# Row halves of an M2 tile between the score bursts of the first three quads

## The chip, the cores and the metric

The kernel runs on one core of a Trainium2 chip. The metric is the device time of one execution in microseconds (us); shorter is better. The core has a matrix engine (TensorE, "PE" in the profile, its weight loads "PEld"), a vector engine (DVE), an activation engine (ACT), a general engine (POOL) and a queue engine (SP). Each works through its own instructions in order, and semaphores tie them together.

## The reference

Attention with a decay, for 8 batches, 8 heads, 576 positions and 64 channels, and behind it a two-layer SiLU network on 4608 tokens of 512 channels:

```python
scores = scale * np.matmul(q, k.transpose(0, 1, 3, 2))
cum = np.cumsum(np.log(np.clip(f, 0.0001, 1.0)), axis=-1)
decay = cum[:, :, :, None] - cum[:, :, None, :]
scores = np.where(causal, -1000000000.0, scores + decay)   # causal: the upper triangle
attn = softmax(scores)
x = (attn @ v)  # as (4608, 512)
h = x @ w_in                       # 512 -> 2048
g = h * (1.0 / (1.0 + np.exp(-h)))
out = g @ w_out                    # 2048 -> 512
```

## The kernel before

**The numbers.** Everything that TensorE multiplies is bf16. The decay is taken apart: V, and a column of ones beside it, are multiplied by a weight per position (`convert_v`, L410, on POOL), so that the exponential of the scaled score, masked, is all that is needed, and the column of ones gives the divisor.

**The stages.** The first 128 positions of every batch are done ahead, up to about 62 us. The other 448 of each batch go by pairs of heads: 4 pairs in a batch, 32 in all. Two pairs are a **quad**; the loop at L952 runs quads m = 0 to 15, and pairs n = 2m and 2m + 1 belong to quad m.

**A pair.** `scores` (L445) is called three times per pair, with c = 0, 1, 2. Each call multiplies K by Q for both heads of the pair into one of two PSUM score buffers, and ACT takes the exponential (L471, L465). The contraction has 64 rows, so one head uses rows 0 to 63 of TensorE and the other rows 64 to 127, at the same time (64\*128 in the profile). Calls 0 and 1 each give one "wide" exp (1024 columns); call 2 gives a "tail" exp (L465, 640 columns) and a "short" one (256 columns). `mask` (L475) and `mask_tail` (L481) zero the upper triangle on DVE. `attend` (L491) multiplies by V into `dn`: 18 matmuls at L507 and 10 at L516 with all 128 rows, then DVE divides (L524, L525). `back` (L532) transposes the output of a whole quad into the layout that the network needs: for quads 3 to 14 by two DMAs of SP, for the others (0, 1, 2 and 15) by seven TensorE transposes (L549) and two copies on DVE (L552, L555).

**The network.** Tokens are in groups of 256, 384 or 512 columns. **M1** (`m1_chunk`, L561): a group has 16 chunks; a chunk is four matmuls into `hp` (L568), a Tanh on ACT (L576) and a product on DVE (L577) into `gt`. **M2** (`m2_part`, L595): 128 tokens are a tile; a tile is four parts of four 512-wide matmuls into `po` (L613), then an eviction on ACT (L623), then a store from POOL's queue. `hp`, `po`, `pr`, `dn` and `tx` share four PSUM buffers; a new one takes the buffer that has been free longest.

**Row halves.** `m2_rows` (L630) does half an M2 tile: 32 matmuls of 64 rows and 256 columns, two at a time, one on each half of TensorE's rows, into two PSUM buffers `pr`. Half 0 and half 1 exchange the two buffers. Between them `m2_fence` (L648) makes DVE read one column of `pr`, and with it half 1 waits for half 0. `m2_out` (L652) evicts by two DVE instructions (L656). Before the change quads 4 to 15 use it.

**The order** around the change is written out in the loop. A quad has three bursts of scores: (n; 0, 1), (n; 2) with (n+1; 0), and (n+1; 1, 2). In the old form `slot` puts M1 chunks and M2 parts behind each burst, and both attends follow. In the row form the halves of one tile stand between the bursts, then come the first attend, some chunks, the second attend and more chunks. `whole` (L905) first ends an M2 tile that is begun, and returns the next one if it can be had whole. `fill` and `plan` choose between M1 and M2 and count their cost as columns; `slot` also issues the stores that were open when it began, and `passed` counts slots, after some of which a group becomes ready for M1. `turn` and `prepare` issue the casts on POOL (L400, L404), the transposes of Q and K (L428) and the loads of later pairs on SP's queue.

Of the kernel before, what the change touches and what calls it, by code (L numbers as in the profile page):

```python
# [18 lines left out]
def kernel(  # L19
# [80 lines left out]
    def xg(g):  # L100
        if g not in xgs:
            tag, bufs = {4 * P: ("x4", 1), 2 * P: ("x2" if g < 3 else "xt", 2), RB: ("x3", 3)}[GW[g]]
            xgs[g] = xpool.tile([P, NCC, GW[g]], BF16, name=tag, tag=tag, bufs=bufs)
        return xgs[g]
# [45 lines left out]
    def head(p, i):  # L150
        return p // 2 * 4 + 2 * i + p % 2
# [337 lines left out]
    BY_DMA = [3 <= m < NQ - 1 for m in range(NQ)]  # L489

    def attend(n):  # L491
        b, p = divmod(n, NP)
        if p % 2 == 0:
            xqs[n // 2] = xqp.tile([P, NGR, 2, D], BF16, name="xr", tag="xr", bufs=3)
        xq = xqs[n // 2]
        u, ut = us.pop(n), uts[n % 4]
        dn = pbig.tile([P, NGR, D + 1], FP32, name="dn", tag="big")

        def vals(kb, i):
            h = head(p, i)  # L500
            return v0[b][:, h, :] if kb == 0 else vbf[b][:, kb - 1, h, :]

        for i in range(2):
            for c in range(1, NM):
                for kb in range(c + 1):
                    o = AT[c, kb]
                    nc.tensor.matmul(  # L507
                        dn[:, i * NR + c - 1, :],
                        lhsT=u[:, i, o : o + P],
                        rhs=vals(kb, i),  # L510
                        start=(kb == 0),
                        stop=(kb == c),
                    )
        for i in range(2):
            for kb in range(NM + 1):
                nc.tensor.matmul(  # L516
                    dn[:, NGR - 1, :],
                    lhsT=ut[:, kb, i : i + 2, :].rearrange("p i t -> p (i t)"),
                    rhs=vals(kb, i),
                    start=(i == 0 and kb == 0),  # L520
                    stop=(i == 1 and kb == NM),
                )
        rec = recp.tile([P, NGR], FP32, name="rec", tag="rec")
        nc.vector.reciprocal(out=rec[:, :], in_=dn[:, :, D])  # L524
        nc.vector.tensor_tensor(  # L525
            out=xq[:, :, p % 2, :],
            in0=dn[:, :, 0:D],
            in1=rec[:, :, None].to_broadcast([P, NGR, D]),
            op=ALU.mult,
        )  # L530

    def back(m):  # L532
        b, c0 = m // 2, m % 2 * 2
        xq = xqs.pop(m)
        g, t0 = TAILS_OF[b]
        xr = xg(REST_OF[b])[:, c0 : c0 + 2, :]
        xt = xg(g)[:, c0 : c0 + 2, :].rearrange("p i t -> p (i t)")[:, t0 * P : (t0 + 1) * P]
        if BY_DMA[m]:
            nc.sync.dma_start_transpose(
                out=xr.rearrange("p i (a q) -> p (i a) q", q=P),  # L540
                in_=xq[:, 0 : 2 * NR, :, :].rearrange("p c w d -> p (c w d)"),
            )
            nc.sync.dma_start_transpose(
                out=xt[:, None, :], in_=xq[:, 2 * NR, :, :].rearrange("p w d -> p (w d)")
            )
            return
        tx = pbig.tile([P, NGR, P], BF16, name="tx", tag="big")
        for c in range(NGR):
            nc.tensor.transpose(  # L549
                tx[:, c, :], xq[:, c, :, :].rearrange("p w d -> p (w d)"), ident_bf[:, :]  # L550
            )
        nc.vector.tensor_copy(  # L552
            out=xr, in_=tx[:, 0 : 2 * NR, :].rearrange("p (i a) q -> p i (a q)", i=2)
        )
        nc.vector.tensor_copy(out=xt, in_=tx[:, 2 * NR, :])  # L555
# [33 lines left out]
    def store(n):  # L589
        n = max(n, 0)  # L590
        for q_, dst, src in stores[:n]:
            q_.dma_start(out=dst, in_=src)  # L592
        del stores[:n]
# [54 lines left out]
    def m2_fence(g, tb):  # L648

        nc.vector.tensor_copy(out=fence[:, :], in_=pos[g, tb][1][:, 0:1])  # L650
# [22 lines left out]
    at = {"m1": 0, "m2": 0, "left": 0.0}  # L673
# [23 lines left out]
    def step(force=0):  # L697

        a, c = at["m1"], at["m2"]
        want = wanted(a, c)  # L700
        if not want:
            return None
        g1 = M1[a][0] if a < len(M1) else NG
        g2 = M2[c][0] if c < len(M2) else NG
        can1 = g1 in ready and not (M1[a][1] == 0 and g1 > g2 + lag["g"])
        can2 = open2["w"] and c < len(M2) and g2 < g1
        kind = force if (force == 1 and can1) or (force == 2 and can2) else want
        if kind == 1:
            if M1[a][1] == 0:
                begin[g1] = (0, c)  # L710
            m1_chunk(g1, M1[a][1])
            at["m1"] += 1
            t = 4 * (GW[g1] / 2.4 + 2.5)
        else:
            m2_part(*M2[c])
            at["m2"] += 1
            t = 4 * (DM / 2.4 + 2.5)
        return t

    def behind():  # L720
        t = sum(4 * (GW[g] / 2.4 + 2.5) for g, _ in M1[at["m1"] :] if g in ready)
        t += sum(4 * (DM / 2.4 + 2.5) for g, _, _ in M2[at["m2"] :] if g in ready)
        return t / 1000
# [158 lines left out]
    def turn(n):  # L882
        if 0 < n < NU - 2:
            cast_qk(n + 2)
            transposes(n + 2)
# [19 lines left out]
    def whole():  # L905

        while at["m2"] < len(M2) and M2[at["m2"]][2] and wanted(at["m1"], at["m2"]):
            t = step(2)
            at["left"] -= t / 1000
        c = at["m2"]  # L910
        while M1[at["m1"]][0] in ready and M1[at["m1"]][1] >= NFC - 4 and M2[c][0] == M1[at["m1"]][0]:
            at["left"] -= step(1) / 1000
        a = at["m1"]
        if c >= len(M2) or M2[c][2]:
            return None
        g1 = M1[a][0] if a < len(M1) else NG
        return M2[c][:2] if M2[c][0] < g1 else None

    LAG, LOW = 13.0, 2.0
    QUAD = [10.9] * (NQ // 2) + [11.7] * (NQ // 2)  # L920

    def spent():
        t = sum(4 * (GW[g] / 2.4 + 2.5) for g, _ in M1[: at["m1"]])
        return (t + at["m2"] * 4 * (DM / 2.4 + 2.5)) / 1000
# [15 lines left out]
    def passed():  # L940
        for x in pending:
            x[0] -= 1
        while pending and pending[0][0] == 0:
            ready.update(pending.pop(0)[1])

    def slot(us_, least=0, ends=(0, 0)):
        n = len(stores)
        fill(us_, least, ends)
        store(n)
        passed()  # L950

    for m in range(NQ):  # L952
        n = 2 * m
        piece = 1.7 if m < 2 else 2.4
        if m == 2:
            assert at["m2"] >= M2_OF[0]
            first_pool.__exit__(None, None, None)
            gpools[0] = ctx.enter_context(tc.tile_pool(name="third", bufs=1))
            lag["g"] = 2
        if m == 4:  # L960
            lag["parts"] = 12
        goal = (spent() if m <= 4 else goal) + QUAD[m]
        rows = whole() if m > 0 and BY_DMA[m - 1] else None
        scores(n, 0)
        scores(n, 1)
        turn(n)
        if m > 0:
            back(m - 1)
            if m % 2 == 0:
                b = m // 2 - 1  # L970
                pending.append([2, [REST_OF[b]] + ([TAILS_OF[b][0]] if b == NM - 1 else [])])
        prepare(n)
        if rows:
            at["m2"] += 4
            m2_rows(*rows, 0)
            m2_fence(*rows)
            mask(n)
            scores(n, 2)
            scores(n + 1, 0)
            turn(n + 1)  # L980
            prepare(n + 1)
            m2_rows(*rows, 1)
            mask_tail(n)
            mask(n + 1)
            scores(n + 1, 1)
            scores(n + 1, 2)
            m2_out(*rows)
            passed()
            attend(n)
            mask_tail(n + 1)  # L990
            slot(1.9, 3)
            attend(n + 1)
            slot(1.8)
            rest(goal)
            at["left"] = 0.0
            continue
        slot(piece, 0, (1, 0))
        mask(n)
        scores(n, 2)
        scores(n + 1, 0)  # L1000
        turn(n + 1)
        prepare(n + 1)
        slot(piece, 0, (1, 0))
        mask_tail(n)
        mask(n + 1)
        scores(n + 1, 1)
        scores(n + 1, 2)
        mask_tail(n + 1)
        slot(piece, 0, (1, 0))
        attend(n)  # L1010
        attend(n + 1)
        slot(min(3.5, max(0.8, behind() - LAG)) if m > 1 else 0.8)
# [39 lines left out]
```

## Time and profile before

| | |
|---|---|
| median of 3 runs | 340.42 us (340.25 to 346.89) |
| the profiled execution | 340.37 us, its span 338.6 us |
| granted TensorE clock, mean | 0.998 |
| M1 matmuls (L568), busy | 123.0 us |
| M2 matmuls (L613 full rows, L639 halves), busy | 93.8 and 46.0 us |
| score matmuls (L460), busy | 27.8 us |

Quads, from the first score of one to the first score of the next, and the busy time of the engines in them:

| quad | from, to (us) | length | PE | DVE | ACT | POOL |
|---|---|---|---|---|---|---|
| 0 | 62.46 to 71.85 | 9.39 | 9.13 | 4.55 | 7.52 | 5.99 |
| 1 | 71.85 to 82.44 | 10.59 | 10.59 | 7.06 | 8.44 | 3.26 |
| 2 | 82.44 to 96.88 | 14.44 | 14.44 | 7.34 | 9.67 | 7.69 |
| 3 | 96.88 to 109.99 | 13.11 | 13.11 | 9.22 | 10.48 | 7.33 |
| 4 | 109.99 to 124.16 | 14.17 | 14.17 | 7.96 | 9.05 | 3.31 |
| 5 | 124.16 to 137.56 | 13.40 | 13.38 | 9.93 | 10.54 | 7.34 |

How to read it: matmuls are pipelined, and the busy time of one reaches over the start of the next, so a TensorE that is "busy" can still be slower than it could be. The distance from one start to the next is what counts. In the chain of waits a line gives the start, the length and what took it; in a timeline it gives the start, the time from the first start to the last end, the engine, the line, the operation, the shape and the count.

### The profile page before, as it was taken

How to read it: one execution, taken by the hardware profiler on the slowest of the kernel's cores; microseconds unless marked ns; L12 is line 12 of the kernel's file. 1: busy time of each engine (PE TensorE's matmuls, PEld its weight loads, DVE VectorE, ACT ScalarE, POOL GpSimd, SP SyncE). 2: the span in 40 equal slices, each digit the busy share in tenths (PEclk: the TensorE clock that was granted, in tenths of full speed). 3: DMA queues.
4: the chain of work that ended last, by engine and by line, in shares of the span. 5: the costliest groups of instructions: out<-in, count | busy, mean ns of one | idle time of the engine just before them, and what ended most of it. 6: DMA issues, size and time to landing. Idle time of an engine off the chain costs nothing.

```text
span 338.6 us, 10066 instructions
## 1 busy us (share of the span) xinstructions
PE 331.8 (98%) x4136; PEld 223.0 (66%) x4136; DVE 193.1 (57%) x423; ACT 216.7 (64%) x389; POOL 131.1 (39%) x227
## 2 busy tenths in 40 slices
PE   8999999999999999999999999999999999999995
PEld 3745665577656767858767796867777685555654
DVE  4765735275467458656656965775685564333330
ACT  5757636676767767848748794875877583344331
POOL 8986317823618227316332721821652000001011
PEclk9999999999999999999999999999999999999999
DMA  8999999999679699979769979797998200101112
GB/s 155 194 186 223 184 199 167 249 205 186 150 182 214 155 205 162 154 174 177 185 149 200 182 136 210 154 201 146 206 157 138 60 33 14 50 33 39 58 58 66
DMA packets 142462, 50.75 MB, mean 150 GB/s; under 512 B 133328, under 2 KB 139728, under 8 KB 142416
## 3 DMA queue, kind: packets, MB, share of 16 engines
q1 hardware_dynamic: 132400, 32.93, 56.4%
q0 software_dynamic: 9856, 17.04, 21.5%
q8 instruction: 32, 0.52, 0.7%
q10 hardware_dynamic: 160, 0.13, 0.1%
q14 instruction: 14, 0.11, 0.1%
HBM read 36.85 MB, written 9.44 MB: 137 GB/s over the span
## 4 chain that ended last, share of the span: by engine, by line
PE 93%; DMA 2%; DVE 1%; ACT 1%; issue 1%; POOL 1%
PE hp L568 36%; PE po L613 25%; PE pr L639 12%; PE sc L460 7%; PE dn L507 6%; PE dn L516 3%; DMA w_in_bf<-in_moe_w_in_dram 2%; PE tp L286 2%; PE wm L233 1%; DVE gt L577 1%; PE tx L549 1%; POOL vf L141 1%; DVE xq L375 0%; PE sc L320 0%; ACT th L576 0%
## 5 line engine op out<-in xcount | busy, mean ns | idle before, releaser
L577 DVE SCALAR_TENSOR_TENSOR gt<-th,hp 128x384 bf16<-128x384 bf16 (+2 forms) x208 | 107.0, 522 | 74.6 <-ACT th L576 66.2
L576 ACT ACTIVATE th<-hp 128x384 bf16<-128x384 f32 (+2 forms) x208 | 96.4, 470 | 73.9 <-PE hp L568 72.3
L568 PE MATMUL hp<-x,w_in_bf 128*128 128x384 bf16 (+2 forms) x704 | 123.0, 321 | 0.9 <-DMA w_in_bf<-in_moe_w_in_dram 0.5
L568 PEld LDWEIGHTS <-w_in_bf 128*128 128x128 bf16 x832 | 78.8, 98 | 49.8 <-issue 0.8
L613 PE MATMUL po<-w_out_bf,gt 128*128 128x512 bf16 (+1 forms) x400 | 93.8, 371 | 0.0
L471 ACT ACTIVATE u<-sc 128x1024 bf16<-128x1024 f32 (+1 forms) x96 | 74.7, 818 | 7.0 <-PE sc L460 7.0
L613 PEld LDWEIGHTS <-gt 128*128 128x128 bf16 x400 | 37.6, 98 | 32.5 <-issue 0.2
L592 POOL DMA_DIRECT2D out_dram<-osb x38 | 20.9, 551 | 87.3 <-ACT osb L623 36.5
L414 POOL TENSOR_TENSOR vp<-vf,w_bf 128x520 bf16<-128x520 f32 (+1 forms) x32 | 34.1, 1067 | 36.7 <-DMA vf<-in_v_dram 30.3
L639 PE MATMUL pr<-w_out_bf,gt 64*128 64x256 bf16 x768 | 46.0, 269 | 0.0
L639 PEld LDWEIGHTS <-gt 64*128 64x128 bf16 x768 | 38.6, 94 | 2.8
L400 POOL CAST qkb<-qf 128x384 bf16<-128x384 f32 x32 | 18.1, 566 | 48.4 <-DMA qf<-in_q_dram 47.7
L623 ACT ACTIVATE osb<-po 128x512 f32<-128x512 f32 (+1 forms) x25 | 14.6, 584 | 26.6 <-PE po L613 22.7
L460 PE MATMUL sc<-qkT 64*128 64x128 bf16 (+1 forms) x640 | 27.8, 206 | 0.3 <-ACT u L471 0.3
L477 DVE TENSOR_TENSOR u<-u,tri 128x768 bf16<-128x768 bf16 x32 | 21.3, 666 | 7.7 <-ACT u L471 7.6
L460 PEld LDWEIGHTS <-qkT 64*128 64x128 bf16 x640 | 20.0, 94 | 8.2 <-issue 6.2
L465 ACT ACTIVATE ut<-sc 128x640 bf16<-128x640 f32 x32 | 22.6, 708 | 1.9 <-PE sc L460 1.7
L400 POOL CAST qkb<-kf 128x384 bf16<-128x384 f32 x32 | 17.5, 545 | 16.5 <-DMA kf<-in_k_dram 16.4
L507 PEld LDWEIGHTS <-u 128*128 128x128 bf16 x576 | 20.6, 98 | 2.9
L507 PE MATMUL dn<-vp,u 128*128 128x65 bf16 x384 | 21.8, 194 | 0.0
L525 DVE TENSOR_TENSOR xr<-dn,rec 128x448 bf16<-128x448 f32 x32 | 20.0, 625 | 1.1
L507 PE MATMUL dn<-v,u 128*128 128x65 bf16 x192 | 20.0, 194 | 0.0
(72 smaller groups left out, 244.0 us busy)
## 6 DMA issues: line engine op xcount, KB each, us to landing
out_dram<-osb POOLq DMA_DIRECT2D x32, 256.0 KB, 3.0
vf<-in_v_dram SPq DMA_DIRECT2D x26, 256.0 KB, 4.7
qf<-in_q_dram SPq DMA_DIRECT2D x64, 96.0 KB, 3.4
kf<-in_k_dram SPq DMA_DIRECT2D x64, 96.0 KB, 3.2
w_in_bf<-in_moe_w_in_dram POOLq DMA_DIRECT2D x4, 512.0 KB, 7.8
w_out_bf<-in_moe_w_out_dram POOLq DMA_DIRECT2D x4, 512.0 KB, 8.4
vf<-in_v_dram POOLq DMA_DIRECT2D x6, 256.0 KB, 9.8
qkb<-in_q_dram POOLq DMA_DIRECT2D x8, 128.0 KB, 5.3
```

Of the source, the lines that this page charges most:

```text
L400: nc.gpsimd.tensor_copy(out=t2[:, c0 : c0 + NR, :].rearrange("p c x -> p (c x)"), in_=t[:, :, :, :].rearrange("p c h d -> p (c h d)"),)
L414: nc.gpsimd.tensor_tensor(out=vbf[b][r, c, :, :], in0=vst[b][c][r, :, :], in1=w_bf[r, c + 1, b * H : (b + 1) * H, None].to_broadcast([n, H ...
L460: nc.tensor.matmul(sc[:, i, o : o + q1 - q0], lhsT=kt, rhs=t[r, q0:q1], start=True, stop=True)
L465: nc.scalar.activation(out=ut[:, :, 0:3:2, :].rearrange("p k i t -> p i k t"), in_=sc[:, :, T0 : T0 + (NM + 1) * ST].rearrange("p i (k t) ...
L471: nc.scalar.activation(out=u[:, :, c * SM : c * SM + w], in_=sc[:, :, 0:w], func=ACT.Exp, scale=scale)
L477: nc.vector.tensor_tensor(out=x, in0=x, in1=tri[:, None, None, :].to_broadcast([P, 2, NR, P]), op=ALU.mult)
L507: nc.tensor.matmul(dn[:, i * NR + c - 1, :], lhsT=u[:, i, o : o + P], rhs=vals(kb, i), start=(kb == 0), stop=(kb == c),)
L568: nc.tensor.matmul(hp[:, :], lhsT=w_in_bf[:, cc, fc * P : (fc + 1) * P], rhs=xcols(g, cc), start=(cc == 0), stop=(cc == NCC - 1),)
L576: nc.scalar.activation(out=th[:, :], in_=hp[:, :], func=ACT.Tanh, scale=0.5)
L577: nc.vector.scalar_tensor_tensor(out=gt[:, fc, :], in0=th[:, :], scalar=1.0, in1=hp[:, :], op0=ALU.add, op1=ALU.mult,)
L613: nc.tensor.matmul(po[:, :], lhsT=gt[:, fc, tb * P : (tb + 1) * P], rhs=w_out_bf[:, fc, m0:m1], start=(fc == 0), stop=(fc == NFC - 1),)
L639: nc.tensor.matmul(pos[g, tb][y], lhsT=gt[r, fc, tb * P : (tb + 1) * P], rhs=w_out_bf[r, fc, y * DM // 2 : (y + 1) * DM // 2], start=(half ...
```

## The change

For quads 0 to 3 the loop now asks `whole` for a tile too. Where it returns one, the quad takes the row form. There `back` of a quad that is transposed by TensorE (`late`) is called behind the first attend and not behind the first burst. In quads 0 and 1 the chunks between and behind the attends are exactly four and two M1 chunks (`ones`, new); in quads 2 and 3 they are chosen by `slot`, and the end of these quads is a slot with a bound of its own. From quad 4 on the written order is the same, and only the share of M1 and M2 in each quad moves.

```diff
@@ -943,6 +943,14 @@
         while pending and pending[0][0] == 0:
             ready.update(pending.pop(0)[1])
 
+    def ones(k):
+        n = len(stores)
+        for _ in range(k):
+            step(1)
+        at["left"] = 0.0
+        store(n)
+        passed()
+
     def slot(us_, least=0, ends=(0, 0)):
         n = len(stores)
         fill(us_, least, ends)
@@ -960,12 +968,14 @@
         if m == 4:
             lag["parts"] = 12
         goal = (spent() if m <= 4 else goal) + QUAD[m]
-        rows = whole() if m > 0 and BY_DMA[m - 1] else None
+        rows = whole()
+        late = bool(rows) and m > 0 and not BY_DMA[m - 1]
         scores(n, 0)
         scores(n, 1)
         turn(n)
         if m > 0:
-            back(m - 1)
+            if not late:
+                back(m - 1)
             if m % 2 == 0:
                 b = m // 2 - 1
                 pending.append([2, [REST_OF[b]] + ([TAILS_OF[b][0]] if b == NM - 1 else [])])
@@ -988,8 +998,19 @@
             passed()
             attend(n)
             mask_tail(n + 1)
-            slot(1.9, 3)
+            if late:
+                back(m - 1)
+            if m < 2:
+                ones(4)
+            else:
+                slot(1.9, 3)
             attend(n + 1)
+            if m < 4:
+                if m < 2:
+                    ones(2)
+                else:
+                    slot(min(5.3, max(0.8, behind() - LAG)))
+                continue
             slot(1.8)
             rest(goal)
             at["left"] = 0.0
```

## The prediction

> **What bounds the kernel now.** The front page comes first.
>
> ```profile
> span 338.6 us, 10066 instructions
> PE 331.8 (98%) x4136; PEld 223.0 (66%) x4136; DVE 193.1 (57%) x423; ACT 216.7 (64%) x389; POOL 131.1 (39%) x227
> ...
> PE 93%; DMA 2%; DVE 1%; ACT 1%; issue 1%; POOL 1%
> ```
>
> TensorE is busy in 98% of the span and carries 93% of the chain that ended last. So the change is worth what it does to the distance from one TensorE instruction to the next, and nothing else, unless another engine makes TensorE wait. The chain of waits gives those distances: first around quad 0, then around quad 4, which already has the new form.
>
> ```profile
> 59.93 0.44 PE hp L568 x4
> 60.37 0.86 PE po L613 x4
> ...
> 62.57 0.58 ACT osb L623
> 63.14 0.82 issue
> 63.96 1.04 ACT u L471
> 65.00 0.04 issue
> 65.05 0.40 PE sc L460 x8
> 65.45 0.97 PE po L613 x4
> ...
> 69.33 0.54 PE dn L507 x18
> ```
>
> ```profile
> 110.06 0.55 PE sc L460 x12
> 110.61 1.75 PE pr L639 x32
> 112.35 0.52 PE sc L460 x20
> 112.87 1.75 PE pr L639 x32
> 114.61 0.42 PE sc L460 x16
> 115.03 0.65 PE dn L507 x18
> ```
>
> The same four `po` take 0.86 after 128-row work and 0.97 after the 64-row scores; eighteen `dn` take 0.54 and 0.65. Leaving 64-row work costs 0.11 us. Entering it shows in the TensorE timeline of quad 0:
>
> ```profile
> 63.01 1.04 PE L613 MATMUL po<-w_out_bf,gt 128*128 128x512 bf16 x4
> 63.88 0.60 PE L568 MATMUL hp<-x,w_in_bf 128*128 128x256 bf16 x4
> 64.42 0.23 PE L460 MATMUL sc<-qkT 64*128 64x128 bf16 x2
> ```
>
> The four `hp` start at 63.88 and the scores at 64.42: 0.54, against 0.44 for four `hp` that other 128-row work follows. Entry costs 0.10. Between two bursts of quad 4 there is only `pr`, also 64 rows, and no such step.
>
> The chain also leaves TensorE in quad 0: the scores at 65.05 wait for the second wide exp (63.96 to 65.00), whose score buffer they need. The last scores before had started at 64.60 and need 0.03, so 0.42 is idle; the next such wait, at 67.11, is 0.11.
>
> **The change, part by part.** The built order shows quads 0 to 2 in the form of quad 4, and quad 3, where no whole M2 tile is left, in the old form with M1 alone between the bursts. From quad 4 on only the share of M1 and M2 in each quad moves.
>
> Mode steps. A quad in the old form enters and leaves 64-row work three times, in the new form once: four steps fewer, 2 x 0.10 + 2 x 0.11 = 0.42, in three quads -1.26 us, all on the path.
>
> Row halves. A tile in halves is 2 x 1.75 = 3.50, against 4 x 0.86 = 3.44 in full rows: +0.06 each, with unrounded starts nearer +0.04, three times +0.12. The page TensorE: Matmul & The Clock Gate (Trainium skill, section Back-to-back issue gap) speaks against this part: it gives a sustained 131 ns for a 512-wide matmul. That would make a full-row tile 16 x 131 = 2.10, and an estimate by it has three tiles costing 3 x 1.40 = 4.2 us more, a slower kernel. The rows have 0.86 / 4 = 0.216 per matmul in every steady stretch, so the measurement is taken.
>
> The waits inside a quad. Quad 0's old idle, 0.42 + 0.11, goes: TensorE now has 1.75 of `pr` instead of 1.30 of work plus steps before that exp is due. The new form has its own wait there. Quad 4 takes 4.98 from its first score (109.99) to its first `dn` (114.97), quad 5 takes 5.08 (124.16 to 129.25); bare work is 3.50 + 0.44 + 0.43 + 0.42 = 4.79 and one step out 0.11, so 0.08 to 0.18 is left. Quad 0, like quad 5, has an eviction (L623) ahead of its exps: 0.18 there and 0.08 in quads 1 and 2. Together -0.53 + 0.34 = -0.19.
>
> Evictions. Three tiles leave by two DVE instructions (L656, 0.74 together in quad 5) instead of one ACT (0.61). DVE is idle behind them there, waiting 0.22 for `dn`; nothing on the path. The fence (L650) holds back the masks (L477) and everything behind them on DVE until the first half is done; quad 4 bears the same, and its `dn` start without a wait.
>
> Four chunks between the two attends, quads 0 and 1. The first `dn` of the second attend needs the PSUM buffer of the first of them. By quad 5's timelines the first Tanh behind the exps starts 6.79 after the quad's first score; with a 256-wide Tanh of 0.38 and its product of 0.42 the buffer is free at about 7.65. TensorE comes at 5.08 + 0.86 + 4 x 0.44 = 7.70. No wait in quad 0. In quad 1 the two copies of the moved transposes (L552 0.56, L555 0.21) stand ahead of the product on DVE: free near 8.0, and the chunks themselves hold for their buffer: +0.1, between 0 and 0.4.
>
> Transposes moved behind the first attend (quads 1 and 2): seven matmuls of 0.40 either way. Their group's first M1 chunk stands three M2 parts and an attend behind them, about 2 us behind the copies. Had it come at once, it would wait those 0.8 us.
>
> Stores and loads. SP's order is unchanged. On POOL the casts for pair 3 now stand ahead of four stores, and a fifth store waits for quad 0's tile, evicted near 68.3; behind it is pair 4's cast, which waited for its load until 69.10 before. About 0.2 us of cover remains, and pair 4's scores come only in quad 2, over 10 us later. Nothing.
>
> Quad 3, the cost. ACT runs in order, and its list there is: two wide exps, two Tanh, the tail exp and the short exp of one pair, a wide exp, four Tanh, a wide exp, tail, short, then Tanh 7. Start to start these take 0.90 (wide: 63.06 to 63.96), 0.39 (384-wide Tanh with the next instruction ready: 96.98 to 97.37), and, by the rows below, 0.58 (tail) and 0.30 (short).
>
> ```profile
> 130.07 0.70 ACT L465 ACTIVATE ut<-sc 128x640 bf16<-128x640 f32 x1
> 130.65 0.39 ACT L471 ACTIVATE u<-sc 128x256 bf16<-128x256 f32 x1
> 130.95 0.49 ACT L576 ACTIVATE th<-hp 128x384 bf16<-128x384 f32 x1
> ```
>
> First exp at +0.60, then 4 x 0.90 + 6 x 0.39 + 2 x 0.58 + 2 x 0.30 = 7.7: Tanh 7 at +8.3, ended at +8.8, its product (0.55) at +9.35. TensorE reaches the first attend after three bursts (0.55, 0.58, 0.53), transposes 0.40, ten chunks of 0.65 and two entries of 0.10: +8.75. Chunks 7 to 10 hold all four PSUM buffers, so the attend waits for product 7: 0.6 us idle. Before, one M2 part and two chunks stood between the third burst and the attend, and no such wait shows. From both sides: 0, as in quad 3 of before; 2.2, as in the third rival. I take 0.6, the sum from the rows.
>
> **Sum.** -1.26 + 0.12 - 0.19 + 0.1 + 0.6 = -0.63 us. The profiled execution took 340.37 (span 338.6 and 1.8 around it), 0.05 below the median of 340.42. Forecast: 339.8.
>
> **Rivals.**
> No hole in quad 3: the queue drains in time and -1.2 remains, 339.2. For it: 0.6 is a small difference between two sums of 9 us. Against: the order on ACT is fixed, and both exps behind the third burst stand ahead of Tanh 7.
>
> Nothing gained, 340.4: the idle simply moves to where ACT and DVE hand back buffers, another 0.3 in quads 1 and 2 each. For it: ACT is busy in 7.5 of 9.4 us of quad 0. Against: quads 4 to 15 live with this form and show 0.1 to 0.2.
>
> Slower: in quad 3 three masks stand ahead of product 7 on DVE, and POOL converts V there (L414). One tail mask met such a conversion in quad 5 and took 1.07 instead of 0.21. Were all three met, DVE is 0.86 + 0.47 + 0.86 = 2.2 later, less 0.6 that it spends waiting anyway: the hole is 2.2, the kernel at 341.4. It decides from a hole of 1.2 on. Against: conversions take 1.05 each and stand apart by their loads, so three hits are unlikely.
>
> **How the numbers follow.** Forecast (339.4 to 340.2) 0.5, no hole 0.25, nothing gained 0.13, slower 0.12. The range: below, no hole and no wait of the new form, 340.4 - 1.26 - 0.53 + 0.12 = 338.7; above, half of the slower case, 340.9. Two per cent, 6.8 us, is about what a measurement of this kernel can tell from no change (the three runs reach from 340.25 to 346.89); no case above comes near it, so "within 2%" has nearly all of the chance, with 0.02 and 0.03 for what I have not seen.
>
> **What would show it.** In the chain of quads 0 to 2: `pr` x32 at 1.75 twice, one `dn` x18 at 0.65, no `po` at 0.97. First score to first `dn` 5.0 to 5.1. In quad 3: idle of about 0.6 before the first `dn`, with DVE `gt` named as its releaser. Quad 4's first score near 109.4 instead of 109.99. Wrong if that score comes after 110, or if quads 1 and 2 wait for buffers, or if the time is lost behind quad 4, which this sum takes as unchanged.

## The result: 344.78 us, and the profile after

The changed kernel takes 344.78 us (median of 22 executions, 342.01 to 347.69) against 340.40 (339.84 to 346.89): a ratio of 1.0095, 95% interval 1.0068 to 1.0121. That is within 2%, but above the predicted range (338.7 to 340.9), and slower than before where the forecast, 339.8, was faster. The profiled execution took 343.73, span 341.9, which is 3.3 us over the span of before and 1 us under the median.

The front page of the changed kernel: span, busy times, and the chain that ended last.

```profile
span 341.9 us, 10332 instructions
PE 329.8 (96%) x4254; PEld 227.9 (67%) x4280; DVE 196.5 (57%) x432; ACT 217.2 (64%) x386; POOL 130.5 (38%) x227
...
PE 65%; DMA 15%; SPq 10%; POOL 5%; issue 2%; ACT 0%; DVE 0%; POOLq 0%
```

TensorE has fallen from 93% of the chain to 65%. Loads, SP's queue and conversions on POOL now carry 30% of it. The waits view of the same kernel names the places (microseconds in total, times, longest):

```profile
PE sc L460 <- DMA qkT<-qkb: 2.3, 2, 1.5
PE dn L507 <- DVE gt L577: 1.3, 1, 1.3
...
PEld L460 <- DMA qkT<-qkb: 3.4, 3, 1.6
```

The second line is quad 3's hole. The other two are one thing seen on the matmul and on its weight load, and they overlap: scores that wait for the transposed Q and K of their pair. There are three such places; the matmul's row has two of them, because the profile puts the third, 0.74 in quad 6, down to ACT, though pair 13's transpose landed only 0.05 ahead of that score. Before, no score waited for a transpose. The TensorE timeline shows the first place, in quad 4, between the second burst's first half (pair 8) and its second half (pair 9), in the changed kernel and then in the kernel before, where the burst runs on:

```profile
111.96 0.28 PE L460 MATMUL sc<-qkT 64*128 64x64 bf16 x8
113.13 0.40 PE L460 MATMUL sc<-qkT 64*128 64x128 bf16 x8 [0.88 <-DMA qkT<-qkb]
```

```profile
112.24 0.19 PE L460 MATMUL sc<-qkT,kT 64*128 64x64 bf16 x2
112.27 0.59 PE L460 MATMUL sc<-qkT 64*128 64x64 bf16 x16
```

With the bare work of each stretch (every matmul at its steady spacing) taken off, the profiled execution divides like this (a wait or a hole is counted here beyond that spacing, and comes out some 0.1 to 0.2 longer than the idle time that the profile prints):

| stretch | before | after | difference |
|---|---|---|---|
| start to quad 0's first score | 62.46 | 61.94 | -0.52 |
| quad 0's first score to quad 4's | 47.53 | 47.74 | +0.21 |
| of it: bare work | 44.15 | 44.27 | +0.12 |
| of it: the hole in quad 3 | 0 | 1.43 | +1.43 |
| of it: mode steps and other waits | 3.38 | 2.04 | -1.34 |
| quad 4's first score to the end | 228.61 | 232.22 | +3.61 |
| of it: waits for pairs 9, 13, 17 (quads 4, 6, 8) | 0 | 0.97 + 0.83 + 1.54 | +3.34 |

The code ahead of quad 0 is unchanged; over all kernels here that start lies between 61.9 and 63.4 us. So the gain that was forecast in quads 0 to 2 is there, and 4.8 us of new waits stand against it. A further loss that the experiments found, a wait in quad 0, is not in this execution, whose quad 0 takes 9.57.

### The profile page after: what moved, and what is told of

It reads as the page before. It is cut to its first block, busy times and chain, and to the rows that moved or that the text cites. A ratio compares the mean times of both kernels' runs of the same rounds, so it can differ in the third digit from the quotient of the medians.

```text
span 341.9 us, 10332 instructions
## 1 busy us (share of the span) xinstructions
PE 329.8 (96%) x4254; PEld 227.9 (67%) x4280; DVE 196.5 (57%) x432; ACT 217.2 (64%) x386; POOL 130.5 (38%) x227
## 4 chain that ended last, share of the span: by engine, by line
PE 65%; DMA 15%; SPq 10%; POOL 5%; issue 2%; ACT 0%; DVE 0%; POOLq 0%
PE hp L568 25%; PE po L613 16%; PE pr L639 11%; PE sc L460 5%; PE dn L507 4%; DMA vf<-in_v_dram 4%; DMA qkT<-qkb 4%; SPq L159 4%; DMA w_out_bf<-in_moe_w_out_dram 3%; SPq L428 3%; DMA qktf<-in_k_dram 3%; PE dn L516 2%; DMA kf<-in_k_dram 2%; SPq L169 2%; SPq L180 2%
## 5 line engine op out<-in xcount | busy, mean ns | idle before, releaser
L568 PE MATMUL hp<-x,w_in_bf 128*128 128x384 bf16 (+2 forms) x700 | 121.4, 321 | 0.8 <-DVE x L552 0.3
L613 PE MATMUL po<-w_out_bf,gt 128*128 128x512 bf16 (+1 forms) x331 | 77.3, 369 | 1.2 <-issue 0.2
L639 PE MATMUL pr<-w_out_bf,gt 64*128 64x256 bf16 x960 | 57.5, 269 | 0.0
L613 PEld LDWEIGHTS <-gt 128*128 128x128 bf16 x352 | 33.6, 98 | 29.3
L639 PEld LDWEIGHTS <-gt 64*128 64x128 bf16 x960 | 47.6, 94 | 4.0
L623 ACT ACTIVATE osb<-po 128x512 f32<-128x512 f32 (+1 forms) x22 | 12.7, 579 | 24.2 <-PE po L613 24.2
```

The costliest lines, as they stand in the source:

```text
L568: nc.tensor.matmul(hp[:, :], lhsT=w_in_bf[:, cc, fc * P : (fc + 1) * P], rhs=xcols(g, cc), start=(cc == 0), stop=(cc == NCC - 1),)
L613: nc.tensor.matmul(po[:, :], lhsT=gt[:, fc, tb * P : (tb + 1) * P], rhs=w_out_bf[:, fc, m0:m1], start=(fc == 0), stop=(fc == NFC - 1),)
L639: nc.tensor.matmul(pos[g, tb][y], lhsT=gt[r, fc, tb * P : (tb + 1) * P], rhs=w_out_bf[r, fc, y * DM // 2 : (y + 1) * DM // 2], start=(half ...
```

## The experiments

Each experiment's ratio is that to the kernel before on the same chip, with its 95% interval.

**Shares and the hole.** `even` sets the shares of M1 and M2 in quads 4 to 8 back to those of before; `q3` puts quad 3's third slot behind its attends.

```diff
-            rest(goal)
+            rest(goal - {4: 1.3, 6: 1.3, 8: 1.3}.get(m, 0.0))
```

```diff
-        slot(piece, 0, (1, 0))
+        if m != 3:
+            slot(piece, 0, (1, 0))
         attend(n)
         attend(n + 1)
-        slot(min(3.5, max(0.8, behind() - LAG)) if m > 1 else 0.8)
+        slot((min(3.5, max(0.8, behind() - LAG)) if m > 1 else 0.8) + (piece if m == 3 else 0.0))
```

> The changed kernel with the targets of quads 4, 6 and 8 lowered by 1.3 us, which gives quads 4 to 7 the same shares of M1 and M2 as in the kernel before. Theory A (the loss behind quad 3 is a wait of the scores for the DMA transposes of Q and K, and the uneven quads 4 to 8 make it: odd quads of 11 us are too short for SP's queue): the waits of quads 6 and 8 (0.8 and 1.5 us in the profile of the changed kernel) go, that of quad 4 (0.9) stays, 343.6 becomes about 341.3. Theory B (the supply is already late when quad 4 begins, by what was moved on POOL and SP in quads 0 to 2): the lateness is carried on whatever the shares are, 343.6 stays within 0.7.

> The changed kernel with the chunks behind the third burst of quad 3 moved behind both attends, so that no attend waits for the product of chunk 7 (1.4 us idle in the profile of the changed kernel). Theory A and B alike: TensorE arrives 1.4 us earlier at quad 4 and waits there for the transposes of pair 9 that much longer, 343.6 stays within 0.5. Rival C (the hole of quad 3 is itself on the path): 343.6 becomes about 342.2.

`even`: 343.48, ratio 1.0124 (1.0061 to 1.0187), profiled 341.66. Quads 6 and 8 wait 0.36 and nothing, quad 4 still 1.27. The shares decide how much of a late supply is seen; they don't make it late. `q3`: 343.83, ratio 1.011 (1.0068 to 1.0152). Its quad 3 loses 2.6 us, now to masks on DVE, its quad 0 loses 2.1 (explained below), and behind them nothing waits: a quad that is late enough gives the supply its time back. A cure at one place is handed on to the next; single runs with loads can't tell the sizes apart.

**Without the loads.** In the `nl_` kernels Q and K are loaded for pairs 0 to 3 only. The later conversions read what lies in the staging buffers, so what is computed from pair 4 on is of other data. Their line numbers are 4 higher.

```diff
     def load_qk(n):
+        if n >= 4:
+            qst[n] = kept[n % 4]
+            return
...
-        qst[n] = tuple(ts)
+        qst[n] = kept[n] = tuple(ts)
```

> The kernel before without the loads of Q and K from pair 4 on: the casts read the staging buffers of pairs 0 to 3 again, so the output is wrong from there, and 8 DMAs per quad are gone from SP's queue. Theories A and B: the kernel before hardly waits for the supply in its fastest runs, so 340.4 becomes 339.8 to 340.4. Rival C: the same.

> The changed kernel without the loads of Q and K from pair 4 on, as in the run nl_before. Theories A and B (the whole loss behind quad 3 is supply): the waits for transposes, 3.2 us, go, the hole of quad 3 (1.4) stays and the gain of the mode steps (1.2) shows, so it stands within 0.5 us of nl_before, near 340.3. Rival C (the loss lies in TensorE's own order): it stays 2 us or more above nl_before.

`nl_before`: 340.34, all ten within 340.02 to 340.82; ratio 0.9995 (0.998 to 1.001). The kernel before does not wait for these loads on the median, but its scatter upwards goes with them. `nl_after`: 341.68, ratio 1.0017 (0.9987 to 1.0047). No score behind quad 3 waits any more, so the waits there are the Q/K supply. But the ten times fall into groups: 339.98 to 340.27 four times, 341.65 to 342.00 five times, and 344.05. The profile is of the second group. Its quad 0 on DVE, then on POOL, then on TensorE:

```profile
66.66 0.56 DVE L481 TENSOR_TENSOR u<-u,tri 128x768 bf16<-128x768 bf16 x1 [0.89 <-ACT u L475]
69.49 0.75 DVE L660 TENSOR_SCALAR osb<-pr 128x256 f32<-128x256 f32 x2 [2.27 <-DMA out_dram<-osb]
```

```profile
63.73 0.50 POOL L404 CAST qkb<-qf 128x384 bf16<-128x384 f32 x1
64.17 0.51 POOL L404 CAST qkb<-kf 128x384 bf16<-128x384 f32 x1
64.63 0.69 POOL L408 CAST qkb<-qktf 128x128 bf16<-128x128 f32 x1
65.26 2.22 POOL L596 DMA_DIRECT2D out_dram<-osb  x4
```

```profile
69.97 1.72 PE L572 MATMUL hp<-x,w_in_bf 128*128 128x256 bf16 x12 [1.30 <-DVE osb L660]
```

The row tile's eviction needs one of four output buffers. All four hold tiles whose stores were issued from 65.26 on, behind pair 3's conversion. In the kernel before, the same four stood ahead of it:

```profile
63.42 2.22 POOL L592 DMA_DIRECT2D out_dram<-osb  x4
65.68 0.87 POOL L400 CAST qkb<-qf 128x384 bf16<-128x384 f32 x1
```

The first of these stores lands at 69.40 in `nl_after` and at 66.69 in the kernel before. DVE works in order, so the eviction waits 2.27 and everything behind it too, the reciprocal and the products that give PSUM back, and TensorE stops.

**Quad 0's buffer.** `nl_early` issues these four stores ahead of pair 3's conversion, `nl_osb5` has a fifth buffer and leaves the order alone.

```diff
+            if m == 0:
+                store(len(stores))
             turn(n + 1)
             prepare(n + 1)
             m2_rows(*rows, 1)
```

```diff
-    opool = ctx.enter_context(tc.tile_pool(name="opool", bufs=4))
+    opool = ctx.enter_context(tc.tile_pool(name="opool", bufs=5))
```

> The changed kernel without the Q/K loads from pair 4 on, and with one line more: in quad 0 the four waiting output stores are issued before the conversions for pair 3 (as in the kernel before), not behind them. Theory S (the row tile's DVE eviction in quad 0 waits for an output buffer whose store stands behind these conversions on POOL): the wait of about 1.8 us in quad 0 that the same kernel showed without this line is gone, quad 0 is back at 9.5 to 9.6 us, and with quad 3's hole at 0.7 the sum is 338.3 - 1.26 + 0.12 - 0.19 + 0.1 + 0.7 = 337.8 of span, a time of 339.3 to 339.9 against 341.7 without the line. Rival R (the wait in quad 0 is the new form's own, for PSUM or for ACT): 341.5 to 342 as without the line, with the wait in quad 0.

> The changed kernel without the Q/K loads from pair 4 on, with five output buffers in place of four and the stores where the change put them. Theory S (a buffer that the row tile's eviction in quad 0 waits for, because its store stands behind the V conversions and the conversions for pair 3 on POOL): the fifth buffer takes that wait away in every execution, not only in some: one group of times at 339.7 to 340.4, quad 0 at 9.5 to 9.6 us. The same kernel with four buffers had two groups, 340.0 to 340.3 and 341.7 to 342. Rival R (quad 0 waits for something else, such as PSUM or late V conversions): the two groups stay.

`nl_early`: 340.38; seven of ten at 339.60 to 340.56, three at 341.50 to 342.63; ratio 0.9993 (0.9964 to 1.0023). That is three late ones of ten against six: the order alone does not rule the wait out, and whether it makes it rarer is not shown by so few. The stores still stand behind V conversions that wait for V's loads. (The slow three have no profile; `early` below has the wait, its stores issued at 65.92.) `nl_osb5`: 339.92, eleven of twelve within 339.63 to 340.28 (the other, 342.32, with a mean granted clock of 0.993); ratio 0.9975 (0.995 to 1.000). The groups are gone, and quad 0 takes 9.51 instead of `nl_after`'s 11.29: the buffer is the cause. Its quad 3 on DVE also shows what the hole is when POOL stays out of it:

```profile
104.71 0.24 DVE L487 TENSOR_TENSOR ut<-ut,trit 128x128 bf16<-128x128 bf16 x1
104.87 0.55 DVE L481 TENSOR_TENSOR u<-u,tri 128x768 bf16<-128x768 bf16 x1
105.53 0.23 DVE L487 TENSOR_TENSOR ut<-ut,trit 128x128 bf16<-128x128 bf16 x1
106.19 1.95 DVE L581 SCALAR_TENSOR_TENSOR gt<-th,hp 128x384 bf16<-128x384 bf16 x4 [0.43 <-ACT th L580]
```

In the changed kernel the same four instructions, with POOL converting V from 104.13 to 106.64:

```profile
104.41 0.85 DVE L483 TENSOR_TENSOR ut<-ut,trit 128x128 bf16<-128x128 bf16 x1
105.18 0.55 DVE L477 TENSOR_TENSOR u<-u,tri 128x768 bf16<-128x768 bf16 x1
105.65 1.07 DVE L483 TENSOR_TENSOR ut<-ut,trit 128x128 bf16<-128x128 bf16 x1
106.64 1.93 DVE L577 SCALAR_TENSOR_TENSOR gt<-th,hp 128x384 bf16<-128x384 bf16 x4
```

Two tail masks of 0.23 take 0.85 and 1.07, and the hole is 1.43 instead of 0.69.

**With the loads: stores and the conversions of pairs 9, 13, 17.** `early` and `early_even` are the line on the stores, alone and with the shares of `even`. `cf` moves all V conversions of a batch on POOL behind the Q/K conversion of that batch's second pair (9, 13, 17); `cf_osb5` adds the fifth buffer, `cf_osb5_ee` that, the line on the stores and the shares.

```diff
-            for c in range(2 * (p - 2), 2 * (p - 1)) if b > 0 else range(NM * (p - 2)):
+            for c in range(NM * (p - 2)):
                 convert_v(b + 1, c)
```

> The changed kernel with that line alone (loads kept, uneven shares kept). Theory S with supply: quad 0 never waits, stores no longer meet the loads of pairs 4 and 5 on their way, so the conversion of pair 5 ends near 75 instead of 77 and the transposes of pair 9 are issued near 106 instead of 108.4; the wait of quad 4 shrinks from 0.9 to under 0.4. Quad 3's hole (1 to 1.4) and waits from the uneven shares in quads 6 and 8 (0.3 to 1 each) stay: 341 to 343, about 1 to 2 us below the changed kernel. Rival L (the loads are simply slow wherever they stand; the earlier quads run into them): supply as late as in the changed kernel and the time unchanged at 343.5 to 345.

> That line, and the shares of quads 4 to 8 set back to those of before. Theory S and A together: only quad 3's hole is left, 340.4 - 0.63 + 0.5 = 340.3 (340 to 341). Rival L: the wait in quad 4 stays at 1 to 1.3 as with even shares alone, 341.5 to 343.5.

> The changed kernel with all four V conversions of a batch behind the conversion of the next batch's second pair (pairs 9, 13, 17 and so on) on POOL, as they already stand for the first batch; nothing else. Theory P (the waits in quads 4, 6, 8 are those for pairs 9, 13, 17, whose Q/K conversion stands behind two V conversions on POOL that wait for V's load): the conversion of pair 9 ends near 103 instead of 108.4, the waits of 0.9, 0.8 and 1.5 behind quad 3 go to under 0.2 each, and where quad 0 does not wait the time is 341 to 341.5; with quad 0's wait in some executions a median of 341.5 to 342.5. Rival D (the transposes are late because the transfers are slow, whatever POOL's order): 344 to 345, with the waits in place.

> That order and five output buffers. Theories S and P together: only quad 3's hole is left over the prediction's sum, 340.4 - 0.63 and 0.1 to 0.8 more for the hole: 340 to 340.6. If one of them is wrong its waits stay: 341.5 to 343.

> Both, the stores of quad 0 ahead of pair 3's conversions, and the shares of quads 4 to 8 as before. If S and P are the whole cause, the shares and the order of the stores no longer matter: 340 to 340.6, as with both alone. If it is clearly below them, the uneven shares cost something apart from the waits.

| kernel | median | ratio, interval |
|---|---|---|
| `early` | 344.93 | 1.0099, 1.0064 to 1.0134 |
| `early_even` | 343.69 | 1.0071, 1.0039 to 1.0103 |
| `cf` | 342.84 | 1.0064, 1.0033 to 1.0095 |
| `cf_osb5` | 342.83 | 1.0031, 0.9996 to 1.0065 |
| `cf_osb5_ee` | 342.34 | 1.0038, 1.0004 to 1.0072 |

All miss. `early` has quad 0's wait and a hole of 2.8 in its profile. In `cf` pair 9's conversion ends at 106.1 instead of 108.4, but its transposes are issued at 110.4, later than before the edit: on SP they stand behind the loads of pair 10, and these behind pair 8's transposes and four V loads. The theory that pair 9's conversion is held up by two V conversions is right about POOL and wrong about what ends last; the lateness is already there at pair 6.

**Where the supply gets late.** `osb5` is the base (the changed kernel with the fifth buffer). `hold` puts POOL's order up to 85 us back to that of before: the line on the stores, and quad 0's row tile stored only behind quad 1's V conversions. `c6` puts pair 6's conversion ahead of the V conversions of the second batch; `hold_c6_ee` is both, with the shares.

```diff
-    def ones(k):
+    def ones(k, out):
...
-        store(n)
+        store(n if out else 0)
...
-                ones(4)
+                ones(4, m > 0)
...
-                    ones(2)
+                    ones(2, m > 0)
```

```diff
             cast_qk(n + 2)
             transposes(n + 2)
+        if n == NP:
+            for c in range(NM):
+                convert_v(1, c)
...
-        if p >= 2:
-            for c in range(2 * (p - 2), 2 * (p - 1)) if b > 0 else range(NM * (p - 2)):
+        if p >= 2 and b > 0:
+            for c in range(2 * (p - 2), 2 * (p - 1)):
```

> The changed kernel with five output buffers in place of four, nothing else: the base of the next two. Quad 0 without a wait in every execution; the waits behind quad 3 stay (0.7 to 1.5 each for pairs 9, 13, 17): 342 to 344, against 342 to 347.7 for the changed kernel.

> The same, with the four waiting stores ahead of pair 3's conversion and the fifth (quad 0's row tile) held back behind the V conversions of quad 1, so that POOL's order up to 85 us is that of the kernel before. Theory F (the fifth store among the loads makes the supply late): the conversion of pair 5 ends near 75.5 instead of 77.2, pair 6's transposes go out near 88 instead of 90, pair 9's near 106; the waits behind quad 3 are under 0.3 each, 340 to 341. Rival pace (the loads' own pace): pair 6 at 90 and the waits as in osb5, 342 to 344.

> The base with pair 6's conversion ahead of the V conversions of the second batch on POOL. Theory Q (SP's queue idles some 5 us before pair 6's transposes, because their conversion stands behind V conversions that wait for V's loads): pair 6's transposes go out at 82 to 85 instead of 90, all that follows on SP is 3 to 5 us earlier, pair 9's near 105; no waits behind quad 3, 340 to 341. Rival pace: SP's queue and the transfers are full anyway, pair 9's transposes are issued at 107.5 to 108.5 as before, 342 to 344.

> Fifth buffer, stores as before, pair 6 ahead, and the shares of quads 4 to 8 as before. If F or Q holds: the prediction's sum with a hole of 0.7 to 1, 339.8 to 340.3 in nearly all executions, at or slightly below the kernel before. Rival pace: 341 to 343 with waits for pairs 9, 13 and 17 left.

| kernel | median | ratio, interval | pair 6's, pair 9's transposes issued | waits behind quad 3 |
|---|---|---|---|---|
| before | | | 87.9, 105.9 | none |
| changed | 344.78 | 1.0095, 1.0068 to 1.0121 | 90.0, 108.4 | 0.97, 0.83, 1.54 |
| `osb5` (profiled at 347.00) | 343.76 | 1.0076, 1.0037 to 1.0115 | 91.9, 109.2 | 0.54, 0.33, 4.9 |
| `hold` | 342.43 | 1.0029, 0.9994 to 1.0065 | 89.7, 107.2 | none |
| `c6` | 342.39 | 1.0018, 0.9983 to 1.0053 | 86.2, 105.4 | none |
| `hold_c6_ee` | 341.76 | 1.0027, 0.9996 to 1.0058 | 85.6, 104.5 | none |

The SP queue of the changed kernel around pair 6, then of the kernel before and of `c6`:

```profile
83.95 1.02 SPq L159 DMA_DIRECT2D kf<-in_k_dram  x2
90.03 1.25 SPq L428 DMA_TRANSPOSE qkT<-qkb  x1
```

```profile
82.19 1.02 SPq L159 DMA_DIRECT2D kf<-in_k_dram  x2
87.91 1.25 SPq L428 DMA_TRANSPOSE qkT<-qkb  x1
```

```profile
85.09 1.02 SPq L159 DMA_DIRECT2D kf<-in_k_dram  x2
86.22 1.25 SPq L428 DMA_TRANSPOSE qkT<-qkb  x1
```

In the changed kernel SP stands still for 5 us, with later pairs' loads behind it, until pair 6 is converted. It stood still before too, from 83.2 to 87.9, and went on 2.1 us earlier. On POOL that conversion waits behind four V conversions and a store (81.72 to 88.77), and two of the four V loads for these were themselves issued behind pair 5's late transposes (78.45, before 76.86). In `c6` the conversion ends at 79.8 and SP goes on. So theory Q holds for the supply. It did not give its 340: in the profiles of `hold` and `c6` the idle of quad 3's hole is 2.76 and 2.47 (1.27 in the changed kernel), because V conversions and pair 9's casts meet the masks there. Theory F got its times only in part: in `hold` pair 5's conversion ends at 76.2 (75.5 expected), pair 6's transposes are issued at 89.7 (88) and pair 9's at 107.2 (106). DVE in `hold`:

```profile
104.49 1.06 DVE L483 TENSOR_TENSOR ut<-ut,trit 128x128 bf16<-128x128 bf16 x1
105.48 0.55 DVE L477 TENSOR_TENSOR u<-u,tri 128x768 bf16<-128x768 bf16 x1
105.94 2.35 DVE L483 TENSOR_TENSOR ut<-ut,trit 128x128 bf16<-128x128 bf16 x1
108.21 1.94 DVE L577 SCALAR_TENSOR_TENSOR gt<-th,hp 128x384 bf16<-128x384 bf16 x4
```

Their late quad 3 hides part of what is late: TensorE reaches quad 4 3.0 us later in `hold` than in the changed kernel, and 2.6 later in `c6`. Without its waits the changed kernel would have asked for pair 9 at 112.2 and for pair 17 at 167.3. The transposes of pair 9 land at 110.7 in `hold` and 108.7 in `c6`, in time for that; those of pair 17 at 168.0 and 167.7, not quite. The fair pair is `hold_c6_ee` and `even`, which have the same shares. In `hold_c6_ee` TensorE asks no later (pair 9 at 112.45 against 113.03, pair 13 at 140.0 against 141.0, pair 17 at 167.6 against 168.6), and the transposes land 4.2, 2.7 and 1.8 us ahead of their scores, against 0.04, 0.04 and 0.11. So with the fifth buffer, the order on POOL takes these waits away without a late TensorE. With the fifth buffer a smaller wait for the supply shows earlier: 0.35 to 0.57 in quad 1 for pair 3's transposes, in the profiles of `osb5`, `cf_osb5` and `cf_osb5_ee`.

**Versions.** `c01` has the row form in quads 0 and 1 only, with the line on the stores and the shares; `c01_hold_c6` adds the rest of `hold_c6_ee`. `b_c6` is the kernel before with the edit of `c6` alone.

```diff
-        rows = whole()
+        rows = whole() if m < 2 or BY_DMA[m - 1] else None
```

> Both, and only quads 0 and 1 in the row form: quads 2 and 3 as before, with M2 parts between their bursts, so no hole in quad 3; from quad 2 on every engine's order is that of before. By the terms of the prediction for two quads: -0.84 + 0.08 - 0.27 + 0.1 = -0.93: 339.5 (339.2 to 339.9). Rival L: the quads reach the loads earlier and wait for them: 340.3 to 341.

> As hold_c6_ee, but only quads 0 and 1 in the row form; quads 2 and 3 are those of before, with M2 parts between their bursts. If quad 3's ten chunks of M1 are what lets conversions and masks on POOL and DVE reach TensorE, its hole shrinks to 0.5 or less, no wait behind: two quads' terms of the prediction, -0.93, and 0.5 to 1 for waits in quads 2 and 3 as in c01: 339.6 to 340.5 with little scatter. If the scatter stays (341 to 344), something beside the hole and the supply makes it.

> The kernel before with pair 6's conversion ahead of the V conversions on POOL. If the scatter of the kernel before (339.7 to 346) is its own Q/K supply running late in some executions, this narrows it to 339.8 to 341, with the median 0.3 to 0.8 below; without these loads it took 340.0 to 340.8. If the scatter comes from elsewhere: the same median and scatter as the kernel before.

`c01`: 341.82, ratio 1.0014 (0.9986 to 1.0041). No waits behind quad 3, but 0.46 and 0.51 lost in quads 2 and 3. `c01_hold_c6`: 341.01, ratio 0.9986 (0.9958 to 1.0015), not told apart from before. `b_c6`: 340.05, all twelve within 339.88 to 340.56; ratio 0.9954 (0.9931 to 0.9978), while the kernel before scattered from 339.70 to 344.55 beside it. It is not faster than before's best executions; it removes their tail. It is the one version here that beats both kernels, and it has nothing of the change in it. In its profile pair 9's transposes are issued at 105.7, no earlier than before's 105.9, so how it removes the tail is not shown; the profile of before is one of its good executions.

## Why the prediction was wrong

**Mode steps, row halves, waits inside a quad, four chunks: right.** Predicted -1.26 + 0.12 - 0.19 + 0.1; measured +0.12 of bare work and -1.34 for the rest, against -1.35. A step into or out of 64-row work takes 0.106 in every profile here. The 131 ns for a 512-wide matmul that the Trainium skill gives (TensorE: Matmul & The Clock Gate, Back-to-back issue gap) shows nowhere: the bare work of quads 0 to 3 grew by 0.12, not by 4.2. The moved transposes cost nothing in quads 1 and 2, as predicted.

**Quad 3: right mechanism, mis-sized term.** 0.6 was taken; where POOL is not converting V beside the last masks (`nl_osb5`) it is 0.69, in the profiled execution 1.43, in others up to 2.8. The third rival had the mechanism and its price (2.2), and called three hits unlikely because conversions "stand apart by their loads". Two hits were enough, and when the loads moved, so did the conversions. One hit can also cost more than the 0.86 of that rival: in `hold` one tail mask took 2.35, through pair 9's casts and a conversion. The price should have stood in the forecast as a spread and not at its lower end.

**"Stores and loads ... Nothing": wrong, the first failed step.** It saw that pair 3's conversion now stood ahead of four stores, and priced that by what POOL does next. Who waits for the stores was not asked: the row tile's eviction, on DVE, for a buffer that they hold, with all of DVE's list behind it. The same omission is in "nothing on the path" for the evictions. `nl_osb5` shows it: with one buffer more one group of times is left, and 1.8 us of quad 0 are gone. In the changed kernel itself the profiled execution has 0.52 of this wait on DVE and none on TensorE; its share in the median of 344.78 was not measured.

**"From quad 4 on only the share of M1 and M2 in each quad moves": wrong, and the larger part.** The sum took the rest of the kernel as unchanged: 3.34 us of waits too few, and some 0.25 more that comes with the moved shares even where nothing waits (`nl_osb5` takes 228.86 from quad 4's first score to the end, `nl_before` 228.63). The prediction had named time lost behind quad 4 as a sign of being wrong, and had put no term on it. `nl_after` shows that the waits are the Q/K supply. "About 0.2 us of cover remains" for pair 4's conversion was correct as far as it went, but the slack was counted only to the next use of that pair, 10 us away. The queues pass a delay on: pair 5's conversion ended at 77.2 instead of 75.1, pair 6's at 90.0 instead of 87.9, pair 9's at 108.4 instead of 105.9, while TensorE reached quad 4 only 0.3 earlier. What first makes pairs 4 and 5 late stays open: `hold` has the old order on POOL there and still ends pair 5 at 76.2, and `b_c6`, whose order up to there is that of the kernel before, ends it at 76.6, so single executions differ by 1.5 us at that place. At pair 6 the difference is firmer, though only one profile stands on the other side: its transposes were issued at 89.4 to 91.9 in all eleven profiles of the changed kernel and its versions that have the loads and not the edit of `c6`, and at 87.9 in the kernel before. From 60 to 220 us the DMA engines have a mean share of 94% in the kernel before and of 68% in `nl_osb5`, so with the loads there is probably little room to catch up. `c6` and `hold_c6_ee` show that the lateness can be taken out at pair 6.

With the fifth buffer and without the loads, `nl_osb5` is at 339.92. In its profile the way from quad 0's first score to quad 4's takes 47.05, in that of `nl_before` 47.52: -0.47 where -0.63 was forecast. The arithmetic on TensorE's side was sound to 0.16, and the error was to treat the other queues as having slack because nothing waited for them yet.

**The scatter.** Twelve of the changed kernel's 22 executions have a mean granted clock of 0.988 to 0.995, and these are twelve of its thirteen slowest. In single executions the new waits are long enough to lower TensorE's clock, as the last section shows; with a mean clock of 0.995, 0.5% of 342 us is 1.7 us. That this is the whole difference between the profiled 343.73 and the median was not shown.

## What to carry to other kernels

An instruction that is moved past a store moves the release of the store's buffer: follow the buffer to whoever fills it next, and then that engine's whole list. Where a chain of loads, conversions and transposes runs through in-order queues, "needed only 10 us later" is not slack; compare the chain's issue times pair by pair up to the tightest use, and ask which queue stands still and behind what. If two engines slow each other in a stage that another edit shifts in time, price that stage by its worst profile too, and a meeting by what is left of the other engine's work when it begins.

## What the hardware showed

An idle of 2.5 to 3.3 us cost more than itself. TensorE's timeline of `hold` at the end of its hole, and then the windows of the same stretch (its columns: the stretch, its length, the busy time of PE, PEld, DVE, ACT and POOL, and then the granted clock, the DMA share and GB/s):

```profile
108.81 0.21 PE L507 MATMUL dn<-v,u 128*128 128x65 bf16 x1 [2.76 <-DVE gt L577]
```

```profile
108.00:108.80 0.80, 0.00 (x0) 0.00 (x0) 0.80 (x3) 0.00 (x0) 0.72 (x2) 0.91 1.07 240
108.80:109.80 1.00, 0.99 (x19) 0.99 (x19) 1.00 (x3) 0.49 (x1) 0.94 (x2) 0.50 1.31 166
109.80:110.80 1.00, 1.00 (x22) 1.00 (x20) 0.57 (x3) 0.00 (x0) 0.78 (x3) 0.50 0.70 158
110.80:111.80 1.00, 1.00 (x22) 1.00 (x20) 0.61 (x1) 0.00 (x0) 0.00 (x0) 0.50 0.85 195
111.80:112.80 1.00, 1.00 (x13) 0.48 (x12) 0.68 (x2) 0.00 (x0) 0.00 (x0) 0.86 0.26 51
112.80:113.80 1.00, 1.00 (x24) 0.87 (x24) 0.61 (x2) 0.99 (x2) 0.51 (x1) 1.00 0.98 181
```

The clock is at half for some 3.4 us, and the attend's stretch took 4.4 us more than its work and its mode step, 1.7 more than the idle. The same followed an idle of 2.47 in `c6` and of 3.27 in `osb5`, and did not follow 2.65 in `early`. The Trainium skill, page TensorE: Matmul & The Clock Gate (Part 1), has the clock halved after at least one idle window of about 3.4 us, and lets the window run freely. The halving, its length and the missing reproducibility agree with these traces; that it takes a whole idle window does not, since 2.47 us were enough here.

A DVE tail mask was as slow as the POOL work that it met. The 20 profiles hold 640 tail masks behind 62 us. The 351 that no cast or V conversion on POOL touched took 0.21 to 0.23. Of the 248 that began while one was running, 202 ended 0.07 to 0.09 after that POOL instruction did, however much of it was left. 33 kept their 0.21 to 0.23 because so little of it was left that this comes to the same, and 2 kept them without such a reason. The other 11 ran on through several POOL instructions in a row, up to 2.22; the 2.35 in `hold` began just ahead of such a row. The wider mask takes 0.54 to 0.56 by itself; of 193 that began beside a running POOL instruction, 161 ended 0.40 to 0.42 after it. In the changed kernel's fence above it began as one conversion ended and kept its 0.55, and the conversion that began beside it took 1.35 instead of 1.05. So the 0.85 and 1.07 there are what was left of two conversions. That POOL holds the mask back, and not a third thing both, is read off these rows; no run tested it apart.
